# An attention and routed-MLP kernel: an eighth buffer for ScalarE's tiles, output rows scaled on GpSimd, another plan, and the routed rows stored by plain DMAs

## The chip, the cores and the metric

The kernel runs on one core of a Trainium2 chip. The metric is the device time of one execution in microseconds (us). The engines are TensorE (PE, with its weight loads as PEld), VectorE (DVE), ScalarE (ACT), GpSimd (POOL) and SyncE (SP, which here only issues DMAs).

## The reference

One transformer layer on 2048 rows of width 448 in bfloat16: attention with 16 heads that share one key and one value head of width 28, then an MLP that is applied to eight rows alone.

```python
def _A_ref(x, wq, wk, wv, wo):
    B, S, D = x.shape            # 1, 2048, 448
    H = 16; Dh = D // H          # 28
    q = (x @ wq).reshape(B, S, H, Dh).transpose(0, 2, 1, 3)
    k = x @ wk                   # one key head, one value head
    v = x @ wv
    scores = jnp.einsum("bhqd,bkd->bhqk", q, k) * (Dh ** -0.5)
    p = _softmax(scores, axis=-1)
    o = jnp.einsum("bhqk,bkd->bhqd", p, v)
    return o.transpose(0, 2, 1, 3).reshape(B, S, H * Dh) @ wo

def _B_ref(x, w_r, w_gate, w_up, w_down):
    r = x @ w_r
    idx = jnp.argsort(-r, axis=-1)[:, :8]          # eight rows with the largest r
    x_sel = the rows idx of x
    y = (_silu(x_sel @ w_gate) * (x_sel @ w_up)) @ w_down      # F = 1792
    y = y * _sigmoid(r[idx])
    return x + (y added to the rows idx)

h  = x + _A_ref(_layernorm(x), ...)
h2 = h + _B_ref(_layernorm(h), ...)
```

## The kernel before

**How the order comes about.** The program first collects all operations in a graph (`_Graph.op`), each with its engine, an assumed duration, a priority `prio`, and the tiles that it reads and writes. `_Graph.plan` then plays the engines through in that model and fixes the order of every engine's instructions. `emit` writes them out, with a semaphore wait wherever an operation needs one of another engine. On the chip each engine keeps to its order, so an instruction that waits holds all that stand behind it on its engine.

Two rules of `plan` matter here. On TensorE, the score products for ScalarE are marked `crit`. When one of them is due soon, another piece of work (a filler) may start before it only if it would end at most `SLACK` ns after the product is due; otherwise TensorE waits for the product if it is due within `WAIT` ns, and else starts a filler all the same:

```python
fit = [o for o in now if t + o.dur + 100.0 * (o.form != form) <= soon.ready + SLACK]
if fit:
    c = min(fit, key=lambda o: (o.prio, o.idx))
elif soon.ready - t < WAIT:
    c, s = soon, soon.ready
```

And operations that are called `lock` (some of VectorE's) are kept apart in time from those of GpSimd, all of which count as `lock`; a GpSimd operation also waits for the last such VectorE operation.

**The work.** There are 16 blocks (four groups of four heads by four groups of 512 query rows), each with 16 tiles of 128 keys. For a tile, TensorE makes scores into two pairs of PSUM banks (`qk`), an engine turns them into weights, and TensorE multiplies these with the values into the block's accumulator. Which engine does the weights is fixed by `TILES` (per block: its VectorE tiles, how many of them give one step to GpSimd, and an offset in time) and by `EARLY` for the first two blocks:

- A ScalarE tile is two pieces (`act_unit`). Each is one exponential of 128x1024 scores from PSUM into one of `NPB` buffers of `P` (L1012). One product with the values takes two buffers (`act_pv`). The score banks 0 and 1, 2 and 3 alternate.
- A VectorE tile is two pieces (`dve_unit`, L1024) from the banks 4 and 5, which write an integer form of the weights into `Y`, and three shifted copies of it (`shift`, L1031). The third copy goes to GpSimd for the first tiles of a block, as many as `TILES` says. Its product with the values (`dve_pv`) has four times as many matmuls as that of a ScalarE tile.

Beside these run, in the same loop: the projection of the next block's queries (`q_project`), of the keys and values of later rows (`chunk`), the normaliser of the last block by way of DRAM (`post_block`, its product with the output on GpSimd in L767), and for each 128 finished rows the output projection and the second layer norm (`out_proj`). For the row tiles 0 to 7 `out_proj` ends with the scaled output row (L802, VectorE) and a store of two row tiles. All matmuls are recorded under L436, so they are told apart by their operands.

**The tail.** After the last exponential come the last normaliser, projection and layer norm, the search for the eight rows, the gathering of their inputs by one-hot products, the MLP, and the eight new rows in `fin` (two half copies, L1236 on ScalarE and L1238 on VectorE). GpSimd then stores them with one indirect DMA (L1239), whose row numbers `idxc` lie on eight partitions. It waits for the earlier stores of output rows. Every engine also loads a flag into a register (L1284) and branches on it (L1295).

Of the kernel before, what the change touches and what calls it, by code (L numbers as in the profile page):

```python
# [12 lines left out]
I32 = mybir.dt.int32  # L13
U32 = mybir.dt.uint32
F16 = mybir.dt.float16

SLACK, WAIT = 248.0, 240.0
# [4 lines left out]
    2: ((0, 5, 8, 13), 4, -0.95),  # L22
    3: ((0, 3, 6, 10, 13), 3, 0.94),
    4: ((2, 8, 10, 12), 2, 1.48),
    5: ((1, 4, 6, 11), 0, 1.34),
    6: ((2, 6, 11, 13), 2, -0.37),
    7: ((1, 3, 8, 11, 13), 2, 1.13),
    8: ((4, 9, 11, 13), 0, 1.08),
    9: ((5, 7, 12), 3, 0.03),
    10: ((0, 5, 8, 10, 12), 3, 1.5),  # L30
    11: ((2, 4, 9, 12), 1, -0.68),
    12: ((0, 2, 4, 8), 4, 0.5),
    13: ((0, 2, 6, 9, 11), 5, 0.63),
    14: ((2, 10, 12), 3, 1.18),
    15: ((0, 4, 8, 10), 1, 0.33),
# [3 lines left out]
EARLY = [(0, 5, 18.21), (0, 15, 22.04), (0, 4, 23.54), (1, 12, 28.01)]  # L39
QUERY = {2: 12.3, 3: 12.3, 4: 6.9, 5: 7.0, 6: 11.5, 7: 11.1, 8: 8.7, 9: 10.4, 10: 6.7, 11: 9.5, 12: 10.1, 13: 7.6}  # L40
ROWS = {
    (0, 0): 10.9, (0, 1): 7.3, (0, 2): 10.3, (0, 3): 9.3, (1, 0): 10.7, (1, 1): 11.9, (1, 2): 13.1,
    (1, 3): 9.9, (2, 0): 6.2, (2, 1): 11.4, (2, 2): 8.4, (2, 3): 9.2
}
CHUNK = (0.0, 5.1, 10.9, 36.9)
# [7 lines left out]
class _Graph:  # L53
# [221 lines left out]
    def emit(self, eng, e, at=None):  # L275
        for o in self.orders[eng]:
# [9 lines left out]
            if w and not o.dma:  # L286
                hold = w.pop()
# [13 lines left out]
def _main(nc, G, sb, ps, psb, flag, scr, xs, ptab, A_x, A_wq, A_wk, A_wv, A_wo, B_w_r, B_w_gate, B_w_up, B_w_down, out,  # L301
# [8 lines left out]
    NPB = 6  # L310
# [12 lines left out]
    idi = sb("idi", [128, 128], I32)  # L323
# [45 lines left out]
    junk = sb("junk", [128, D], BF16)  # L369
    outf = x_sb[:, :, 0:D]  # L370
# [36 lines left out]
    idxc = sb("idxc", [8, 1], U32)  # L407
# [12 lines left out]
    eg = sb("eg", [128, NFC, 8], F32)  # L420
    sg = sb("sg", [128, NFC, 8], F32)
# [10 lines left out]
    def pk(b):  # L432
        return ("ps", b)
# [31 lines left out]
    G.op(PO, lambda e: e.iota(idi[:, :], [[1, 128]], base=0, channel_multiplier=-1), 250, writes=["idi"])  # L465
    G.op(PO, lambda e: e.tensor_single_scalar(ident[:, :], idi[:, :], 0, ALU.is_equal), 560,
         reads=["idi"], writes=["ident"])
# [40 lines left out]
    def kk(j, p):  # L508
        return ("K0", min(j, 2), p) if j < 4 else ("K", j // 4, p)
# [25 lines left out]
    def late_consts(gate):  # L535
# [16 lines left out]
        G.op(PO, lambda e: e.memset(onesb[:, :], 1.0), 200, writes=["onesb"])  # L552
        G.op(PO, lambda e: e.memset(bz[:, :, :], 0.0), 100, writes=["bz"])
        G.op(PO, lambda e: e.memset(onesh[:, :], 1.0), 200, writes=["onesh"])
# [6 lines left out]
        G.op(PO, lambda e: e.iota(idi[0:8, 0:96], [[1, 96]], base=0, channel_multiplier=0), 250, writes=["idi"])  # L561
        G.op(PO, lambda e: e.tensor_copy(iota96[:, :], idi[0:8, 0:96]), 300, reads=["idi"], writes=["iota96"])
# [7 lines left out]
        G.op(PO, lambda e: e.iota(idi[:, :], [[-32, 4], [0, 32]], base=0, channel_multiplier=1), 250, writes=["idi"])  # L570
# [209 lines left out]
    def out_proj(qb, k):  # L780
# [20 lines left out]
        if qb < 2:  # L801
            G.op(DV, lambda e: e.tensor_scalar(outf[:, t, :], h, st[:, t, 5:6], s6, ALU.mult, ALU.add), 420,  # L802
                 reads=[("h", hr), ("st5", t), ("h6", hr)], writes=[("outf", t)], lock=True)
# [216 lines left out]
    def dve_unit(m, b, j, p, t):  # L1020
        n = m % NY
        G.op(PE, qk(4, b, j, p), 216, reads=[("Q", b % 4), ("Qh", b % 4), kk(j, p)], writes=[pk(4), pk(5)], prio=t - 2.9,
             form=1)
        G.op(DV, lambda e: e.tensor_scalar(Y[:, n, 0, p:p + 3:2, :].bitcast(I16), ps[:, 4:6, :], 0.0,  # L1024
                                           32639.0 - 3 * STEP, ALU.max, ALU.min), 1140, reads=[pk(4), pk(5)],
             writes=[("Y", n, 0, p)], prio=t - 2)

    def shift(m, v, b):
# [18 lines left out]
    for m, (b, j, t) in enumerate(dve_tiles):  # L1047
        for p in range(2):
            at(t + 1.5 * p, dve_unit, m, b, j, p, t + 1.5 * p)
        for v in (1, 2, 3):  # L1050
            at(t + 1.6 + 0.5 * v, shift, m, v, b)
# [295 lines left out]
```

## Time and profile before

| | |
|---|---|
| time, median of 3 runs | 388.7 us (387.9 to 390.82) |
| time of the profiled execution | 387.67 us |
| its span, first to last instruction | 385.9 us |
| granted TensorE clock, mean | 0.984 |
| ScalarE busy | 374.1 us |
| TensorE busy | 344.0 us |
| VectorE busy | 338.2 us |
| GpSimd busy | 115.0 us |

How to read the lines. In a group of instructions stand the line of the kernel, the engine, the operation, output and input with their shapes, the count, then the busy time of the group, the mean duration of one instruction in ns, and the engine's idle time just before them with what ended it. Instructions overlap on an engine, so the busy time can be less than count times duration. The chain that ended last is followed back from the last instruction, and shown in order of time as start, duration and what ran. In the timeline a row has the start, the time from first start to last end of the merged instructions (x12 is twelve), and in brackets the idle time before them. A "q" behind an engine's name is its sequencer, which issues DMAs and loads registers. The row of a window gives its ends, its length, and the busy time and count of PE, PEld, DVE, ACT and POOL. An answer on one line gives for each engine the count, then the shortest, median and longest duration in ns, then the start of the first and of the last.

### The profile page before, as it was taken

The page shows a single profiled execution, that of the slowest core. Times are in us where ns is not written, and L with a number is a line of the kernel's source. Part 1 is how long each engine was busy: PE and PEld are TensorE (multiplying, and loading weights), DVE is VectorE, ACT ScalarE, POOL GpSimd, SP SyncE. Part 2 cuts the span into 40 slices and gives each one's busy share as a digit, 9 for nine tenths or more (in the row PEclk, how much of TensorE's full clock was granted, in tenths as well). Part 3 has the DMA queues.
Part 4 walks back from the last instruction along what each step waited for, and adds up shares of the span by engine and source line. Part 5 has one row for each costly group of instructions (what it writes and reads, how often), then busy time and mean ns, then how long its engine had stood idle before and what let it go on. Part 6 is the DMA issues. An engine that isn't in the chain of part 4 may idle for free.

```text
span 385.9 us, 8129 instructions
## 1 busy us (share of the span) xinstructions
PE 344.0 (89%) x3361; PEld 105.6 (27%) x3361; DVE 338.2 (88%) x613; ACT 374.1 (97%) x433; POOL 115.0 (30%) x149
## 2 busy tenths in 40 slices
PE   7799898989988999899998988999898999888945
PEld 7333222222222222222222222222222222222324
DVE  6985888888998999989999989999999998999382
ACT  6999999999999999999999999999999999999992
POOL 7440002544123112404101244402145454431100
PEclk9999999999999999999999999999999999999985
DMA  8696000100000000201001000011001010100011
GB/s 208 163 235 190 2 2 12 49 2 29 2 27 5 4 29 26 77 1 54 2 14 63 7 27 27 28 50 31 26 30 51 3 53 27 52 26 20 14 51 55
DMA packets 18045, 17.12 MB, mean 44 GB/s; under 512 B 6660, under 2 KB 15124, under 8 KB 18004
## 3 DMA queue, kind: packets, MB, share of 16 engines
q1 hardware_dynamic: 17652, 16.32, 14.7%
q8 instruction: 27, 0.44, 0.5%
q10 hardware_dynamic: 288, 0.23, 0.2%
q14 instruction: 14, 0.11, 0.1%
q0 software_dynamic: 64, 0.02, 0.0%
HBM read 11.70 MB, written 4.86 MB: 43 GB/s over the span
## 4 chain that ended last, share of the span: by engine, by line
ACT 92%; PE 3%; DVE 3%; DMA 1%; issue 0%; SPq 0%; POOL 0%; POOLq 0%
ACT P L1012 90%; PE ps L436 3%; DMA wq_sb<-in_A_wq_dram 1%; ACT xn L964 1%; DVE Y L1024 1%; DVE topb L856 0%; DVE bn L934 0%; SPq L449 0%; ACT x_sb L825 0%; DVE Y L1031 0%; ACT xnT L618 0%; POOL out_dram L1239 0%; ACT Rb L741 0%; ACT Rb L739 0%; ACT wq_pad L491 0%
## 5 line engine op out<-in xcount | busy, mean ns | idle before, releaser
L1012 ACT ACTIVATE P<-ps 128x1024 bf16<-128x1024 f32 x388 | 356.3, 1132 | 1.4 <-PE ps L436 1.3
L436 PE MATMUL ps<-Q,K 64*128 64x512 bf16 x1024 | 179.9, 385 | 29.3 <-ACT P L1012 25.0
L1024 DVE TENSOR_SCALAR Y<-ps 128x1024 int16<-128x1024 f32 x124 | 151.2, 1219 | 19.8 <-PE ps L436 19.5
L1031 DVE TENSOR_SCALAR Y<-Y 128x2048 int16<-128x2048 int16 x153 | 100.4, 685 | 0.5
L436 PEld LDWEIGHTS ps<-Q,K 64*128 64x128 bf16 x1024 | 44.7, 93 | 175.4 <-ACT P L1012 152.7
L1031 POOL TENSOR_SCALAR Y<-Y 128x2048 int16<-128x2048 int16 x33 | 62.6, 1898 | 96.4 <-DVE Y L1031 87.6
L436 PE MATMUL ps<-Y,Vs 128*32 128x512 bf16 x992 | 84.9, 383 | 0.0
L436 PE MATMUL ps<-P,Vs 128*32 128x512 bf16 x776 | 76.3, 388 | 0.1
L767 POOL TENSOR_TENSOR On<-Ot,Rb 128x512 bf16<-128x512 f32 x15 | 19.1, 1273 | 45.5 <-DVE Y L1031 30.6
L436 PEld LDWEIGHTS ps<-Y,Vs 128*32 128x32 bf16 x992 | 23.8, 95 | 27.3 <-issue 17.5
L436 PEld LDWEIGHTS ps<-P,Vs 128*32 128x32 bf16 x776 | 19.6, 93 | 42.5 <-issue 41.7
L763 POOL TENSOR_TENSOR Ls<-Ls,Lc 128x16 f32<-128x16 f32 x15 | 4.2, 280 | 68.2 <-DVE Y L1031 60.9
L436 PE MATMUL ps<-xnT,wq_pad 112*128 112x512 bf16 (+1 forms) x68 | 19.2, 371 | 0.6 <-DVE K L643 0.5
L436 PE MATMUL ps<-wo_pad,On 128*128 128x448 bf16 (+1 forms) x64 | 17.5, 358 | 1.0 <-DVE On L745 1.0
L517 DVE TENSOR_SCALAR Q<-ps,qone 128x512 bf16<-128x512 f32 x15 | 11.0, 734 | 1.7 <-PE ps L436 1.7
L795 POOL TENSOR_TENSOR hbuf<-st,nhalf 128x1 f32<-128x1 f32 x12 | 6.6, 552 | 14.3 <-DVE Y L1031 10.3
L751 DVE COPY Ot<-ps 128x512 f32<-128x512 f32 x15 | 10.3, 684 | 0.7 <-PE ps L436 0.4
L804 DVE SCALAR_TENSOR_TENSOR junk<-hbuf,w_rb 128x448 bf16<-128x448 f32 x12 | 8.1, 677 | 0.0
L789 DVE TENSOR_TENSOR hbuf<-ps,x_sb 128x448 f32<-128x448 f32 x12 | 7.4, 618 | 0.3 <-PE ps L436 0.2
L791 DVE BATCH_NORM_STATS2 bn<-hbuf 128x6 f32<-128x448 f32 x12 | 7.4, 618 | 0.1
L719 DVE TENSOR_SCALAR K<-ps,ksc,kb 128x512 bf16<-128x512 f32 x6 | 4.6, 803 | 3.3 <-PE ps L436 3.3
L1239 POOL DMA_INDIRECT out_dram<-wq_sb,idxc x1 | 0.9, 930 | 20.8 <-DVE wq_sb L1238 20.8
(209 smaller groups left out, 172.1 us busy)
## 6 DMA issues: line engine op xcount, KB each, us to landing
Rb<-h_scr SPq DMA_DIRECT2D x15, 256.0 KB
h_scr<-hbuf SPq DMA_DIRECT2D x12, 225.0 KB, 2.2
out_dram<-x_sb SPq DMA_DIRECT2D x8, 224.0 KB, 2.5
wg_sb<-in_B_w_gate_dram SPq DMA_DIRECT2D x1, 1568.0 KB, 12.2
wu_sb<-in_B_w_up_dram SPq DMA_DIRECT2D x1, 1568.0 KB, 18.7
wd_sb<-in_B_w_down_dram SPq DMA_DIRECT2D x1, 1568.0 KB, 22.1
x_sb<-in_A_x_dram SPq DMA_DIRECT2D x3, 448.0 KB, 5.6
wo_pad<-in_A_wo_dram SPq DMA_DIRECT2D x4, 98.0 KB
```

The source lines that it names most:

```text
L436: return lambda e: e.matmul(o, lhsT=l, rhs=r, start=start, stop=stop)
L517: G.op(DV, lambda e: e.tensor_scalar(Q[:, b % 4, :], ps[:, bank, :], qone[:, 0:1], None, ALU.add), dvt(512), reads=[pk(bank), "qone"], wri ...
L719: G.op(DV, lambda e, bank=bank, c=c, p=p: e.tensor_scalar(K[:, p, c * 512:(c + 1) * 512], ps[:, bank, :], ksc[:, p:p + 1], kb[:, p:p + 1], ...
L751: G.op(DV, lambda e: e.tensor_copy(Ot[:, rb, :], ps[:, acc_bank(b), :]), dvt(512), reads=[pk(acc_bank(b))], writes=[("Ot", rb)], prio=u - 30)
L767: G.op(PO, lambda e: e.tensor_tensor(On[:, qb % 2, g, :], Ot[:, rb, :], Rb[:, rb, :], ALU.mult), 1270, reads=[("Ot", rb), ("Rb", rb)], wri ...
L789: G.op(DV, lambda e: e.tensor_tensor(h, ps[:, bank, 0:D], x_sb[:, t, 0:D], ALU.add), dvt(D), reads=[pk(bank), ("x", t)], writes=[("h", hr)])
L791: G.op(DV, lambda e: e.bn_stats(bn6[:, t, :], h), dvt(D), reads=[("h", hr)], writes=[("bn6", t)])
L795: G.op(PO, lambda e: e.tensor_tensor(s4, st[:, t, 7:8], nhalf[:, 0:1], ALU.pow), 570, reads=[("st7", t), "nhalf"], writes=[("h4", hr)])
L804: G.op(DV, lambda e: e.scalar_tensor_tensor(junk[:, :], h, s4, w_rb[:, :], ALU.mult, ALU.mult, accum_out=st[:, t, 2:3]), 700, reads=[("h", ...
L1012: marks["exp"] = G.op(AC, lambda e: e.activation(P[:, sl, :, :], ps[:, b0:b0 + 2, :], ACT.Exp, bias=EBIAS, scale=OCT), 905, reads=[pk(b0), ...
L1024: G.op(DV, lambda e: e.tensor_scalar(Y[:, n, 0, p:p + 3:2, :].bitcast(I16), ps[:, 4:6, :], 0.0, 32639.0 - 3 * STEP, ALU.max, ALU.min), 114 ...
L1031: G.op(PO if po else DV, lambda e: e.tensor_scalar(Y[:, n, v, :, :].bitcast(I16), Y[:, n, 0, :, :].bitcast(I16), 1.0, v * STEP, ALU.mult, ...
```

## The change

- `NPB` goes from 6 to 8 buffers of `P`. To make room, `idi` is laid into `junk`, and `onesb`, `onesh`, `eg` and `sg` into `wq_sb`.
- `TILES`, `EARLY`, `QUERY`, `ROWS`, `CHUNK`, `SLACK` and `WAIT` have other values. The VectorE tiles in `TILES` are 60 instead of 58 (with four in `EARLY` each time), and those whose third copy goes to GpSimd are 45 instead of 33. The priorities of `dve_unit` and `shift` get offsets of their own, `PACE`, and the assumed duration of a copy on GpSimd goes from 2030 to 1930 ns.
- The scaled output rows of the row tiles in `POOLROWS` (seven of the eight) are made on GpSimd.
- The eight routed rows are stored by eight plain DMAs, four issued by SP and four by ScalarE. The byte offset of a row is made on one partition (`idxr`), loaded into registers of the two engines (`fetch`, after all earlier stores of output rows), and used as the address (`put`).

```diff
-SLACK, WAIT = 248.0, 240.0
+SLACK, WAIT = 144.0, 159.0
 TILES = {
-    2: ((0, 5, 8, 13), 4, -0.95),
-    3: ((0, 3, 6, 10, 13), 3, 0.94),
...
-    14: ((2, 10, 12), 3, 1.18),
-    15: ((0, 4, 8, 10), 1, 0.33),
+    2: ((0, 2, 6, 12), 4, -1.5),
+    3: ((0, 2, 6, 10, 13), 4, 0.75),
...
+    14: ((0, 3, 7, 11), 2, 0.98),
+    15: ((0, 4, 6, 11), 1, 0.84),
 }
...
+POOLROWS = [0, 1, 2, 3, 4, 5, 7]
+PACE = (-6.4, -1.8, 1.1, -3.6, 1.5, 2.8)
-CHUNK = (0.0, 5.1, 10.9, 36.9)
+CHUNK = (0.0, 6.3, 7.4, 13.5)
...
-            if w and not o.dma:
+            if w and not o.dma and o.name != "load":
                 hold = w.pop()
...
-    NPB = 6
+    NPB = 8
...
-    idi = sb("idi", [128, 128], I32)
+    idi = junk[:, 0:256].bitcast(I32)
-    idxc = sb("idxc", [8, 1], U32)
+    idxr = sb("idxr", [1, 8], I32)
-    onesb = sb("onesb", [128, 128], BF16)
+    onesb = wq_sb[:, 1, 0:128]
-    onesh = sb("onesh", [128, 128], F16)
+    onesh = wq_sb[:, 2, 0:128].bitcast(F16)
-    eg = sb("eg", [128, NFC, 8], F32)
-    sg = sb("sg", [128, NFC, 8], F32)
+    eg, sg = (wq_sb[:, 3, 224 * k:224 * k + 224].bitcast(F32).rearrange("p (c n) -> p c n", n=8) for k in range(2))
...
         if qb < 2:
-            G.op(DV, lambda e: e.tensor_scalar(outf[:, t, :], h, st[:, t, 5:6], s6, ALU.mult, ALU.add), 420,
-                 reads=[("h", hr), ("st5", t), ("h6", hr)], writes=[("outf", t)], lock=True)
+            on = t in POOLROWS
+            G.op(PO if on else DV, lambda e: e.tensor_scalar(outf[:, t, :], h, st[:, t, 5:6], s6, ALU.mult, ALU.add),
+                 900 if on else 420, reads=[("h", hr), ("st5", t), ("h6", hr)], writes=[("outf", t)], lock=True)
...
     def dve_unit(m, b, j, p, t):
-        G.op(PE, qk(4, b, j, p), 216, ..., prio=t - 2.9, form=1)
+        G.op(PE, qk(4, b, j, p), 216, ..., prio=t + PACE[0] + (PACE[2] - 1.5) * p, form=1)
-             writes=[("Y", n, 0, p)], prio=t - 2)
+             writes=[("Y", n, 0, p)], prio=t + PACE[1] + (PACE[2] - 1.5) * p)
-    def shift(m, v, b):
+    def shift(m, v, b, t):
-                                  1.0, v * STEP, ALU.mult, ALU.add), 2030 if po else 605,
+                                  1.0, v * STEP, ALU.mult, ALU.add), 1930 if po else 605,
-             writes=[("Y", n, v)], lock=True)
+             writes=[("Y", n, v)], lock=True, prio=t + PACE[2 + v])
...
-    ps3 = ps[0:8, 2, 480:482]
-    G.op(PE, [mm(ps3, oh5[:, k, :], x_sb[:, 12 + k, D:D + 2], k == 0, False) for k in range(4)] +
-         [mm(ps3, oh5[:, 4, :], extc[:, D:D + 2], False, True)], 200, ...)
-    G.op(DV, lambda e: e.tensor_copy(sel3[:, :], ps3[:, 1:2]), 70, ...)
-    G.op(DV, lambda e: e.tensor_tensor(idxc[:, :], ps3[:, 0:1], sel3[:, :], ALU.add), 70, ...)
+    lrow = ps[0:1, 2, 480:488]
+    G.op(PE, [mm(lrow, (x_sb[:, 12 + k, D + h:D + h + 1] if k < 4 else extc[:, D + h:D + h + 1]), oh5[:, k, :],
+                 k == h == 0, k == 4 and h == 1) for k in range(5) for h in range(2)], 280, ...)
+    G.op(DV, lambda e: e.tensor_scalar(idxr[:, :], lrow, 2.0 * D, None, ALU.mult), 70, ...)
...
-    o = G.op(PO, lambda e: e.indirect_dma_start(out[0], bass.IndirectOffsetOnAxis(ap=idxc[:, 0:1], axis=0),
-                                                fin[:, :], None), 1000, dma=True, ...)
-    evs.append(o)
+    out_b = out[0].rearrange("s d -> (s d)").bitcast(U8)
+    where = {}
+    def fetch(i):
+        def run(e):
+            got = nc.values_load_multi_w_load_instructions(
+                idxr[0:1, i:i + 4], engines=(e.engine,), min_val=0, max_val=(S - 1) * 2 * D, ...)[1]
+            where.update(zip(range(i, i + 4), got))
+        return run
+    def put(j):
+        return lambda e: e.dma_start(out_b[bass.ds(where[j], 2 * D)].unsqueeze(0), fin[j:j + 1, :].bitcast(U8))
+    outs = [("out", q, k) for q in range(4) for k in (1, 3)]
+    for i, eng in ((0, SP), (4, AC)):
+        o = G.op(eng, fetch(i), 500, reads=["idxr"] + outs, prio=329.8)
+        o.name = "load"
+        for j in range(i, i + 4):
+            evs.append(G.op(eng, put(j), 100, dma=True, reads=["fin0", "fin1"], writes=[("out", 4 + j)], prio=331, after=[o]))
```

More of the change, by code (lines that the diff above doesn't have):

```diff
@@ L1238, in _main @@
     G.op(DV, lambda e: e.tensor_copy(fin[:, hd:D], ps[0:8, 1, hd:D]), 300, reads=[pk(1)], writes=["fin1"])
-    o = G.op(PO, lambda e: e.indirect_dma_start(out[0], bass.IndirectOffsetOnAxis(ap=idxc[:, 0:1], axis=0),
-                                                fin[:, :], None), 1000, dma=True,
-             reads=["fin0", "fin1", "idxc"] + [("out", q, k) for q in range(4) for k in (1, 3)],
-             writes=[("out", 4)])
-    evs.append(o)
+    out_b = out[0].rearrange("s d -> (s d)").bitcast(U8)
[3 more added lines that the diff above has]
+            got = nc.values_load_multi_w_load_instructions(
+                idxr[0:1, i:i + 4], engines=(e.engine,), min_val=0, max_val=(S - 1) * 2 * D,
+                skip_runtime_bounds_check_because="a one-hot sum of the bytes ahead of a row below S")[1]
+            where.update(zip(range(i, i + 4), got))
[8 more added lines that the diff above has]
+            evs.append(G.op(eng, put(j), 100, dma=True, reads=["fin0", "fin1"], writes=[("out", 4 + j)], prio=331, after=[o]))
     G.close(evs, "flag")
```

54 lines of the change are left out of this document (26 added, 28 removed).

## The prediction

> **What bounds the kernel now.** I read the page's busy shares, its chain and its groups first, then the chain in order of time.
>
> ```profile
> span 385.9 us, 8129 instructions
> PE 344.0 (89%) x3361; PEld 105.6 (27%) x3361; DVE 338.2 (88%) x613; ACT 374.1 (97%) x433; POOL 115.0 (30%) x149
> ACT 92%; PE 3%; DVE 3%; DMA 1%; issue 0%; SPq 0%; POOL 0%; POOLq 0%
> L1012 ACT ACTIVATE P<-ps 128x1024 bf16<-128x1024 f32 x388 | 356.3, 1132 | 1.4 <-PE ps L436 1.3
> ```
>
> ScalarE (ACT) is busy 97% of the span, and 92% of the chain that ended last lies on it. Nearly all of that is one group, the exponential of line 1012: 388 pieces, 356.3 us, with 1.4 us of idle time before them. One piece lasts 1132 ns but overlaps its neighbour, so the pace is 356.3 / 388 = 0.918 us. The same view in order of time shows how whole this is:
>
> ```profile
> 9.47 59.75 ACT P L1012 x65
> 69.23 121.64 ACT P L1012 x133
> 190.91 148.97 ACT P L1012 x162
> ...
> 349.28 16.61 ACT P L1012 x18
> ```
>
> From 9.47 to 365.89 us ScalarE does exponentials and nothing else. What follows, up to 385.9, is a serial tail of 20.0 us. Once, between 339.88 (190.91 + 148.97) and 349.28, the chain leaves ScalarE, for PE and DVE. The remaining 388 - 378 = 10 pieces run there, in 9.40 us.
>
> The other engines in this loop, one row for the whole of it (PE, PEld, DVE, ACT, POOL busy), and ScalarE in its last undisturbed stretch:
>
> ```profile
> 9.47:365.88 356.41, 326.33 (x3033) 91.41 (x3031) 320.99 (x533) 356.27 (x389) 106.97 (x116) 1.00 0.14 40
> 355.68 10.20 ACT L1012 ACTIVATE P<-ps 128x1024 bf16<-128x1024 f32 x11
> ```
>
> DVE has 356.4 - 321.0 = 35.4 us to spare, PE 30.1, POOL 249. The stretch gives a pace of (10.20 - 1.13) / 10 = 0.907 us. So 388 x (0.918 - 0.907) = 4.3 us of the loop is score matmuls that came a little late.
>
> **The change, part by part.** *Fewer exponentials.* The key tiles on VectorE go from 62 (58 in the table, 4 early) to 64 (60 and 4). Each of the 256 tiles is two score pieces, so ScalarE has 384 instead of 388: 4 x 0.918 = **-3.67 us**, wholly on the path. The price is paid beside it:
>
> ```profile
> L1024 DVE TENSOR_SCALAR Y<-ps 128x1024 int16<-128x1024 f32 x124 | 151.2, 1219 | 19.8 <-PE ps L436 19.5
> L1031 DVE TENSOR_SCALAR Y<-Y 128x2048 int16<-128x2048 int16 x153 | 100.4, 685 | 0.5
> L1031 POOL TENSOR_SCALAR Y<-Y 128x2048 int16<-128x2048 int16 x33 | 62.6, 1898 | 96.4 <-DVE Y L1031 87.6
> L436 PE MATMUL ps<-Y,Vs 128*32 128x512 bf16 x992 | 84.9, 383 | 0.0
> L436 PE MATMUL ps<-P,Vs 128*32 128x512 bf16 x776 | 76.3, 388 | 0.1
> L436 PE MATMUL ps<-wo_pad,On 128*128 128x448 bf16 x48 | 13.1, 358 | 0.0
> L802 DVE TENSOR_SCALAR x_sb<-hbuf,st 128x448 bf16<-128x448 f32 x8 | 4.1, 508 | 0.0
> L699 POOL TENSOR_SCALAR xn<-x_sb,nmean,rstd 128x448 bf16<-128x448 bf16 x5 | 3.5, 713 | 1.1 <-DVE xn L695 0.8
> L767 POOL TENSOR_TENSOR On<-Ot,Rb 128x512 bf16<-128x512 f32 x15 | 19.1, 1273 | 45.5 <-DVE Y L1031 30.6
> ```
>
> DVE gets 4 more L1024 (4 x 151.2 / 124 = +4.9 us). The third shift of a tile goes to GpSimd for 45 tiles instead of 33, so DVE does 3 x 64 - 45 = 147 shifts instead of 153 (6 x 100.4 / 153 = -3.9) and GpSimd 12 more (12 x 1.898 = +22.8). PE gets 32 more Y products and 8 fewer P products (32 x 0.086 - 8 x 0.098 = +2.0 us), against 30.1 of idle time.
>
> *Output rows on GpSimd.* Seven of the eight L802 leave DVE: -3.6 us there. No row shows this operation on GpSimd with f32 input. From below stands L699 (the same operation and width, bf16 in, 0.713), from above L767 (two f32 inputs, 512 wide, 1.273). I take 0.8, near L699, which is alike in all but the input: 7 x 0.8 = +5.6. In the loop DVE comes to 318.4 and GpSimd to 135 of 352 us, so neither is near full and I cost both at nothing. A row that ends later delays its store on SP's queue, and behind that store stand the normaliser's transfers, which feed L767. PE stood idle for 0.0 us before the projections that read it (`wo_pad,On` above). If that cover went, 4 stores times the 0.3 us by which 0.8 exceeds 0.508 would cost 1.2 us.
>
> *Eighth buffer.* A P buffer comes free when its P product has run. At the end of the loop this row stands, just as the exponentials end:
>
> ```profile
> 365.85 0.61 PE L436 MATMUL ps<-P,Vs 128*32 128x512 bf16 x8
> ```
>
> Eight products are two tiles, four buffers: of six, two are free even there, and the page names only 1.3 us in which an exponential waited for PE at all. So the buffers take no wait away: 0. They let the plan put P products later, which belongs to the next part.
>
> *The plan.* PE's order is fixed beforehand. A filler (a product, a projection piece) may start if it would end no more than SLACK after the next score piece is due, 0.248 us before and 0.144 after. Otherwise PE idles if that piece is due within WAIT (0.240, now 0.159), else the filler starts all the same. Short fillers will therefore overrun less, long ones more often. How late a score then comes no row shows. From below all 4.3 us go, with 384 x 0.907. From above stands the rival on long pieces. I stay near the present pace and take **-0.6**, a seventh of that sum.
>
> *The tail.* What now follows the last copies:
>
> ```profile
> 381.16 0.35 ACT L1236 ACTIVATE wq_sb<-ps 8x224 bf16<-8x224 f32 x1 [2.77 <-PE ps L436]
> 381.50 0.38 DVE L1238 CAST wq_sb<-ps 8x224 bf16<-8x224 f32 x1 [0.44 <-PE ps L436]
> 382.45 0.93 POOL L1239 DMA_INDIRECT out_dram<-wq_sb,idxc  x1 [20.80 <-DVE wq_sb L1238]
> out_dram<-wq_sb,idxc POOLq DMA_INDIRECT x1, 2.9
> 2.77 0.49 SPq L449 DMA_DIRECT2D wv_sb<-in_A_wv_dram  x1
> 3.30 0.49 SPq L449 DMA_DIRECT2D wq_sb<-in_A_wq_dram  x1
> h_scr<-Li SPq DMA_DIRECT2D x15, 8.0 KB, 1.4
> Lc<-h_scr SPq DMA_DIRECT2D x16, 8.0 KB, 1.7
> h_scr<-hbuf SPq DMA_DIRECT2D x12, 225.0 KB, 2.2
> ```
>
> The rows are ready at 381.88. The indirect store begins 0.57 later and lands at 382.45 + 2.9 = 385.35, 0.5 before the end. Instead SP and ScalarE issue four stores each, one every 3.30 - 2.77 = 0.53 us, the last at 381.93 + 3 x 0.53 = 383.5. Landing takes 1.4 to 2.2 us by the small and the large transfers; with 1.7 it is 385.2: **-0.2**, bounds -0.5 and +0.3. No row shows a DMA whose address comes from a register. The addresses must be in registers by then, and the load of them waits for all earlier stores. On ScalarE the last copy L1236 stands behind that load; on SP only its own four stores do.
>
> ```profile
> L1284 ACTq TENSOR_LOAD <-flag x1: 552/552/552, 378.2 to 378.2; - x1
> L289 POOLq EVENT_SEMAPHORE  x31: 17/17/4824, 3.8 to 379.4; - x31
> ```
>
> GpSimd's wait for those same stores ends at 379.4. One load of 0.552 ends at 380.0, inside L1236's idle time of 2.77; four loads would end at 381.6 and push the copy 0.45 us late, but the copy beside it ends at 381.88 anyway, so at most +0.1. A register step ahead of each store is bounded by the 17 ns of a semaphore step in the second row and by a whole load, 0.552: four of them add 0.1 to 2.2 us on a queue. I take the first, since a step on registers moves no data, and it stays inside the rounding of -0.2; the upper bound of the tail becomes +2.6. The row index now takes ten small matmuls instead of five and one DVE step instead of two, while PE waits for the selected rows: nothing. The tiles laid into others' memory cost nothing, since each old use is long over.
>
> *The sum.* -3.67 - 0.6 - 0.2 = -4.5 us against the profiled execution's own 387.67, which lies 1.0 below the median of the runs, 388.7. The median after is **384.2**. A change under 1% (3.9 us) can't be told from none.
>
> **Rivals.** *The late scores go too*: with SLACK smaller, ScalarE runs at 0.907 all through. 388.7 - 3.67 - 4.3 - 0.2 = **380.5**. For it speaks that PE has idle time; against it that the long pieces stay long.
>
> *The plan eats the gain.* A long piece holds PE for about 0.54 us:
>
> ```profile
> 66.31 0.61 PE L436 MATMUL ps<-xnT,wq_pad 112*128 112x512 bf16 x2
> 66.85 0.39 PE L436 MATMUL ps<-Q,K 64*128 64x512 bf16 x2
> L436 PE MATMUL ps<-xnT,wq_pad 112*128 112x512 bf16 x60 | 18.2, 384 | 0.5 <-DVE K L643 0.5
> ```
>
> With WAIT smaller it may start 0.08 us nearer to a due score. These 60 and the 48 of `wo_pad,On` are 54 such pieces: 54 x 0.08 = +4.3, so 388.7 - 3.67 - 0.2 + 4.3 = **389.1**, no change. Against it: it wants every piece to meet the worst place.
>
> *GpSimd holds VectorE* (the slower side). A DVE instruction that meets a running GpSimd one can stand still until that ends:
>
> ```profile
> 344.45 1.90 POOL L1031 TENSOR_SCALAR Y<-Y 128x2048 int16<-128x2048 int16 x1 [3.11 <-DVE Y L1031]
> 344.54 1.83 DVE L856 CAST topb<-top 1x8 bf16<-1x8 f32 x1
> 347.42 0.15 DVE L857 CAST posf<-idx 1x8 f32<-1x8 uint32 x1
> ```
>
> A cast of eight numbers took 1.83 us, until GpSimd's shift was over; its neighbour took 0.15. This is where the chain left ScalarE, whose ten pieces took 9.40 instead of 9.07: 0.33 us lost. GpSimd will have 52 shifts and rows instead of 33. From 12 such collisions on (3.9 / 0.33) the gain is gone, from 24 the kernel is over 1% slower; with 26, half of them, 388.7 - 3.9 + 8.6 = **393.4**. Against it: the plan keeps the instructions that it calls `lock` apart, and among 33 shifts only this undeclared cast was caught whole. [...]
>
> *The stores queue up.* If SP's and ScalarE's issues took turns, the eighth would start at 381.93 + 7 x 0.53 = 385.6 and land at 387.3, 2.0 after today's: 388.7 - 4.3 + 2.0 = **386.4**. Against it stand two queues at work at once at the start, each at 0.44 us an issue:
>
> ```profile
> 0.84 0.88 SPq L449 DMA_DIRECT2D x_sb<-in_A_x_dram  x2
> 0.72 0.89 ACTq L449 DMA_DIRECT2D x_sb<-in_A_x_dram  x2
> ```
>
> [...]
>
> **How the numbers follow.** The forecast has 0.48 (its own range 382.5 to 386.5), late scores gone 0.18, gain eaten 0.18, GpSimd's hold 0.11, queued stores 0.05. Faster by over 1% (below 384.8) is 0.18 and two thirds to three quarters of 0.48: 0.52. Slower by over 1% is most of GpSimd's case: 0.10. Within 1%: 0.38. The range reaches from 380.0, under the second case, to 390.0, over the third, and leaves out most of the fourth.
>
> **What would show it.** L1012 x384 at 0.915 to 0.918 us; L1031 x147 on DVE and x45 on POOL, L1024 x128, one L802-like group x7 on POOL near 0.8 us; the last landing within 0.5 us of 3.3 after the copies, with no GpSimd step. A pace over 0.925 says that the plan or GpSimd took the gain: casts or shifts on DVE well over their medians name GpSimd, long pieces ahead of late scores the plan. A load of registers that holds L1236, or eight stores strictly in turn, would prove the tail wrong.

## The result, and the profile after

The changed kernel takes **385.4 us** (median of 4 runs, 384.72 to 385.91) against 388.6 before on the same chip: a ratio of 0.9922, interval 0.990 to 0.9944. That is 3.2 us, or 0.8%. The profiled execution took 385.39 us, 2.28 less than the one of before. From the page of the changed kernel come its span, busy shares, granted clock in 40 slices, the chain's shares and five groups:

```profile
span 383.6 us, 8231 instructions
PE 355.0 (93%) x3390; PEld 105.4 (27%) x3390; DVE 340.0 (89%) x603; ACT 370.3 (97%) x429; POOL 141.2 (37%) x166
PEclk9999999999996999999999999999999999999975
ACT 92%; PE 5%; DVE 1%; issue 0%; POOL 0%; POOLq 0%
L1014 ACT ACTIVATE P<-ps 128x1024 bf16<-128x1024 f32 x384 | 352.6, 1195 | 1.8 <-PE ps L438 1.8
L1026 DVE TENSOR_SCALAR Y<-ps 128x1024 int16<-128x1024 f32 x128 | 155.8, 1217 | 17.9 <-PE ps L438 16.3
L1033 POOL TENSOR_SCALAR Y<-Y 128x2048 int16<-128x2048 int16 x45 | 85.4, 1898 | 103.7 <-DVE Y L1033 103.7
L1033 DVE TENSOR_SCALAR Y<-Y 128x2048 int16<-128x2048 int16 x147 | 100.6, 709 | 0.7
L804 POOL TENSOR_SCALAR x_sb<-hbuf,st 128x448 bf16<-128x448 f32 x7 | 5.0, 715 | 15.5 <-DVE Y L1033 12.3
```

ScalarE is still what bounds the kernel: 97% busy, 92% of the chain. There are 384 exponentials, and their pace, 352.6 / 384 = 0.918 us, is that of before. New is a slice of the clock row that reads 6, or 0.6 of full speed. Before, the row had no such slice ahead of the tail:

```profile
PEclk9999999999999999999999999999999999999985
```

The chain of the changed kernel in order of time shows what lies there:

```profile
9.55 14.77 ACT P L1014 x16
24.34 63.35 ACT P L1014 x69
87.70 30.36 ACT P L1014 x33
118.07 0.05 issue
118.11 2.15 PE ps L438 x10
120.28 1.03 ACT P L1014
121.31 0.05 issue
121.36 3.00 PE ps L438 x16
124.38 68.50 ACT P L1014 x75
192.91 24.18 ACT P L1014 x26
217.09 145.86 ACT P L1014 x159
```

The loop of exponentials runs from 9.55 to 217.09 + 145.86 = 362.95, with a stop near 118 to 124 us where TensorE ends last. Before, the only such stop was at 340. The windows view of the whole loop and of that place (columns: ends, length, busy time and count of PE, PEld, DVE, ACT and POOL, then the granted clock as a share):

```profile
9.55:362.94 353.39, 337.05 (x3057) 91.09 (x3055) 322.65 (x524) 352.64 (x385) 134.08 (x134) 0.99 0.14 40
116.00:126.00 10.00, 8.83 (x58) 1.85 (x62) 9.29 (x16) 9.28 (x11) 2.92 (x2) 0.66 0.07 26
```

The loop took 353.39 us instead of 356.41, so 3.02 less. The granted clock was 0.66 in the 10 us around the stop: full speed fell to half (0.51) from 117.3 to 124.2. Behind the loop, the time to the end grew from 19.97 to 20.64. The rows of the tail (timeline; then the last branch of ScalarE, and the drain that it executes behind it, with count, durations in ns and start):

```profile
375.68 0.65 PE L438 MATMUL ps<-xselT,wu_sb 112*128 112x8 bf16 x19 [0.32 <-issue]
378.67 0.35 ACT L1236 ACTIVATE wq_sb<-ps 8x224 bf16<-8x224 f32 x1 [3.23 <-PE ps L438]
379.42 1.81 ACTq L1251 DMA_DIRECT2D out_dram<-wq_sb  x4
379.41 1.33 SPq L1251 DMA_DIRECT2D out_dram<-wq_sb  x4
L1310 ACTq COMPARE_BRANCH  x1: 72/72/72, 381.3 to 381.3; - x1
L1266 ACTq DRAIN  x1: 66/66/66, 383.3 to 383.3; - x1
```

SP and ScalarE issue their four stores side by side, and the last landing comes at 382.24, 2.85 after the copies, where it was 3.48 before. But the kernel does not end there. ScalarE branches at 381.25 and goes on only at 383.30, so the end lies 1.35 us after the last landing; before it was 0.50. What the stores won was lost again.

### The profile page after: what moved, and what is told of

It reads as the page before. It is cut to its first block, busy times and chain, and to the rows that moved or that the text cites. A ratio compares the mean times of both kernels' runs of the same rounds, so it can differ in the third digit from the quotient of the medians.

```text
span 383.6 us, 8231 instructions
## 1 busy us (share of the span) xinstructions
PE 355.0 (93%) x3390; PEld 105.4 (27%) x3390; DVE 340.0 (89%) x603; ACT 370.3 (97%) x429; POOL 141.2 (37%) x166
## 4 chain that ended last, share of the span: by engine, by line
ACT 92%; PE 5%; DVE 1%; issue 0%; POOL 0%; POOLq 0%
ACT P L1014 91%; PE ps L438 5%; ACT xn L966 1%; DVE bn L936 0%; ACT x_sb L827 0%; PE ps L441 0%; ACT Rb L742 0%; ACT Rb L740 0%; POOL ident L468 0%; DVE On L746 0%; DVE wq_sb L1238 0%; DVE mv L937 0%; POOL junk L467 0%; DVE x_sb L957 0%; DVE Li L756 0%
## 5 line engine op out<-in xcount | busy, mean ns | idle before, releaser
L1014 ACT ACTIVATE P<-ps 128x1024 bf16<-128x1024 f32 x384 | 352.6, 1195 | 1.8 <-PE ps L438 1.8
L1026 DVE TENSOR_SCALAR Y<-ps 128x1024 int16<-128x1024 f32 x128 | 155.8, 1217 | 17.9 <-PE ps L438 16.3
L1033 POOL TENSOR_SCALAR Y<-Y 128x2048 int16<-128x2048 int16 x45 | 85.4, 1898 | 103.7 <-DVE Y L1033 103.7
L1033 DVE TENSOR_SCALAR Y<-Y 128x2048 int16<-128x2048 int16 x147 | 100.6, 709 | 0.7
L438 PE MATMUL ps<-Y,Vs 128*32 128x512 bf16 x1024 | 91.0, 385 | 0.0
L438 PEld LDWEIGHTS ps<-Y,Vs 128*32 128x32 bf16 x1024 | 22.6, 94 | 35.3 <-issue 32.6
L768 POOL TENSOR_TENSOR On<-Ot,Rb 128x512 bf16<-128x512 f32 x15 | 19.1, 1274 | 23.5 <-DVE Y L1033 10.7
L804 POOL TENSOR_SCALAR x_sb<-hbuf,st 128x448 bf16<-128x448 f32 x7 | 5.0, 715 | 15.5 <-DVE Y L1033 12.3
L764 POOL TENSOR_TENSOR Ls<-Ls,Lc 128x16 f32<-128x16 f32 x15 | 3.3, 219 | 20.1 <-DVE junk L896 11.6
```

The source lines that it names most:

```text
L438: return lambda e: e.matmul(o, lhsT=l, rhs=r, start=start, stop=stop)
L768: G.op(PO, lambda e: e.tensor_tensor(On[:, qb % 2, g, :], Ot[:, rb, :], Rb[:, rb, :], ALU.mult), 1270, reads=[("Ot", rb), ("Rb", rb)], wri ...
L804: G.op(PO if on else DV, lambda e: e.tensor_scalar(outf[:, t, :], h, st[:, t, 5:6], s6, ALU.mult, ALU.add), 900 if on else 420, reads=[("h ...
L1014: marks["exp"] = G.op(AC, lambda e: e.activation(P[:, sl, :, :], ps[:, b0:b0 + 2, :], ACT.Exp, bias=EBIAS, scale=OCT), 905, reads=[pk(b0), ...
L1033: G.op(PO if po else DV, lambda e: e.tensor_scalar(Y[:, n, v, :, :].bitcast(I16), Y[:, n, 0, :, :].bitcast(I16), 1.0, v * STEP, ALU.mult, ...
```

## Experiments

**The changed kernel once more**, as the measure for the others.

> The changed kernel itself, beside the kernel before. My theory of the 3 us it gained: four exponentials fewer give -3.67 us, the plan's late scores give and take the same (short fillers -1, long pieces +1), a stretch of lower granted clock near 118 us costs 1.2 us in the profiled execution, and the tail is 0.7 us longer. If the low clock was an accident of that execution, the profile here shows none and a span near 382.4; if it belongs to the new order, it is there again at the same place with a span near 383.6. Median 3 us below before either way.

Measured: 385.83 us (12 runs), ratio 0.9927 [0.9907, 0.9947]. Its profile has a loop of 353.66 and a tail of 20.06, with the clock at half of full speed (half clock, from here on) twice, at 119.3 to 122.8 and 344.6 to 348.0.

**The stores alone**: the tail of before in the changed kernel, one indirect DMA with the row numbers on eight partitions.

```diff
-    for i, eng in ((0, SP), (4, AC)):   # registers, eight stores
+    o = G.op(PO, lambda e: e.indirect_dma_start(out[0], ...))
```

> The changed kernel with the old end: one row index per partition, one indirect DMA on GpSimd; all other engines' orders are the same. Theory: the eight stores land 0.6 us sooner after the copies than the indirect one, but the end of the program then waits about 0.8 us for ScalarE, so the two ends cost the same within 0.3 us: 385.4 +- 0.3. Rival: the longer tail of the changed kernel is the new stores' doing, so this one is 0.7 us faster, 384.7. Second rival: the stores are a gain that something else in the tail hides, so this one is 0.6 slower, 386.0.

Measured: 385.0 us (384.84 to 385.61, 4 runs), ratio 0.9912 [0.9893, 0.9931]. Its tail is 20.04 us, that of the eight stores 20.06 and 20.64 in the two profiles above: the new stores gain nothing over the old one. (The medians are 0.4 to 0.8 us apart, but three of these four runs had a mean clock of 0.979 or more; runs of the changed kernel with such a clock are as fast, see the low clock below.) Its branch needs no 2 us:

```profile
L1297 ACTq COMPARE_BRANCH  x1: 68/68/68, 378.5 to 378.5; - x1
L1253 ACTq DRAIN  x1: 80/80/80, 379.0 to 379.0; - x1
116.00:126.00 10.00, 6.99 (x64) 1.68 (x63) 9.88 (x20) 10.00 (x12) 2.08 (x2) 1.00 0.07 26
```

In the same execution the clock stayed full around 120 us (third row, windows view), and the loop took 352.46, about 1 us less. The edit has no part in that stretch, and the two profiles of the changed kernel differ in their half clock too, so the low clock comes in some executions of this order and not in others.

**Four exponentials twice**: four of the 384 are also written to an unused tile.

```diff
+        twice = (b, j, p) in ((4, 6, 0), (7, 7, 0), (10, 6, 0), (13, 7, 0))
+        fe = [exponential into a spare tile] * twice + [exponential into P]
```

> The changed kernel in its own order, with four of the 384 exponentials (one each in blocks 4, 7, 10 and 13) done twice, the first time into memory that nothing reads then. ScalarE has 388 pieces again, and nothing is taken from VectorE or TensorE. If ScalarE's pieces lie wholly on the path: +4 x 0.903 = +3.6 us on the changed kernel. If part of them is hidden by waits for scores (rival): +1 to +2.5 us.

Measured: 388.32 us (12 runs), ratio 0.9991 [0.9975, 1.0008]. The loop:

```profile
10.15:367.27 357.12, 336.44 (x3057) 90.68 (x3055) 322.15 (x524) 356.32 (x389) 134.30 (x134) 1.00 0.13 39
L1313 ACTq COMPARE_BRANCH  x1: 73/73/73, 385.0 to 385.0; - x1
L1269 ACTq DRAIN  x1: 65/65/65, 385.5 to 385.5; - x1
```

It is 3.73 us over that of the changed kernel and 3.46 over its repetition. Four exponentials are worth 0.87 to 0.93 us each. These loops differ in their half clock; more direct is the start of the piece behind each repeated one, which came 0.90 to 0.93 us late. So they lie wholly on the path. The median rose by 2.5 only; in the profile the tail fell to 19.31, as here ScalarE went on 0.50 us after its branch (384.96 to 385.46). That was not expected, and it became the lead for the end.

**The buffers alone**, eight instead of six, in before's order and with its tail.

```diff
-    NPB = 6
+    NPB = 8        # and the tiles laid into others' memory; plan and tail of before
```

> The kernel before with eight instead of six P buffers and the small tiles laid into others' memory, and nothing else: the order of TensorE, ScalarE, VectorE and SyncE is that of before. Theory: no exponential waited for a buffer, so no change, 388.6 +- 0.4. Rival: buffers were waited for in a few places that the idle time does not show, 0.25 to 0.6 us, or more: 387 to 388.

Measured: 388.49 us (11 runs), ratio 1.0001 [0.9984, 1.0017]. Its loop in the windows view and its exponentials on the page:

```profile
10.10:366.50 356.40, 326.32 (x3033) 91.34 (x3031) 320.79 (x533) 356.27 (x389) 107.39 (x115) 1.00 0.13 39
L1014 ACT ACTIVATE P<-ps 128x1024 bf16<-128x1024 f32 x388 | 356.3, 1134 | 1.4 <-PE ps L438 1.3
```

356.40 against 356.41: without another order the two more buffers are worth nothing.

**Six buffers under the new plan's values.** The planner then has to find its order with six.

```diff
-    NPB = 8
+    NPB = 6
```

> The changed kernel with six P buffers instead of eight, and all else as it is; the plan is made anew for six, with the same numbers. The buffers alone, in the order of before, were worth nothing. If the eight buffers matter only through the order that they allow (theory), this order is worse: an exponential has to find its buffer free, products must come sooner and scores come late, +3 to +7 us on the changed kernel. If they don't matter even so (rival): within 1 us of it.

Measured: 389.06 us (10 runs), ratio 1.0013 [1.0001, 1.0025].

```profile
9.69:366.47 356.78, 332.45 (x3057) 91.62 (x3055) 322.01 (x524) 354.82 (x385) 134.28 (x135) 1.00 0.14 39
```

With 384 exponentials the loop takes 356.78, or 3.4 us more than with eight buffers, spread over some 13 scores late by more than 0.25 us each. So buffers and plan go together: two more remove no wait from the old order, but the new values lose all they gain without them. Values chosen for six buffers and 384 exponentials were not tried, so what the buffers are worth beside the best order with six stays open.

**ScalarE's end, first theory**: the mark that announces the branch, moved from the middle of ScalarE's program to 12 operations before its end.

```diff
-    at = {lst[0 if eng in (PO, SP) else len(lst) // 2].idx: [hint]}
+    at = {lst[0 if eng in (PO, SP) else len(lst) - 12 if eng == AC else len(lst) // 2].idx: [hint]}
```

> The changed kernel with ScalarE's branch hint, which names the target of its last branch, placed 12 operations ahead of ScalarE's end instead of in the middle of its work. In the changed kernel ScalarE goes on 1.8 to 2.05 us after that branch, in the kernel before 0.48, and the program ends with it. If the target has to be fetched anew because the hint is long past (theory), ScalarE goes on 0.5 us after the branch, the end comes 0.5 us after the last landing and the tail is 0.6 to 0.8 us shorter than the changed kernel's 20.06 to 20.64: median 385.1. If ScalarE waits for its own four stores instead (rival), it still goes on 2 us after the branch and nothing changes.

Measured: 385.98 us (6 runs), ratio 0.9931 [0.9915, 0.9947].

```profile
L1310 ACTq COMPARE_BRANCH  x1: 73/73/73, 381.7 to 381.7; - x1
L1266 ACTq DRAIN  x1: 66/66/66, 384.0 to 384.0; - x1
```

The delay is still there (381.67 to 383.97). The theory fell.

**Second theory, the number of ScalarE's stores**: six on SP, two on ScalarE.

```diff
-    for i, eng in ((0, SP), (4, AC)):
+    for i, eng, n in ((0, SP, 6), (6, AC, 2)):
```

> The changed kernel with six of the eight stores on SyncE and two on ScalarE instead of four and four. SyncE's issues came 0.35 us apart, so its last store starts 0.7 us later and lands near 3.4 to 3.5 us after the copies instead of 2.85; ScalarE branches 0.7 us sooner. If ScalarE's late going on sets the end (theory), the end moves with it: 0 to 0.6 us shorter, and the last landing is again 0.5 us ahead of the end. If the last landing sets it (rival): 0.6 us longer.

Measured: 385.88 us (6 runs), ratio 0.9927 [0.9911, 0.9942].

```profile
L1251 ACTq DMA_DIRECT2D out_dram<-wq_sb x2: 249/386/523, 380.0 to 380.9; - x2
L1310 ACTq COMPARE_BRANCH  x1: 72/72/72, 381.2 to 381.2; - x1
L1266 ACTq DRAIN  x1: 66/66/66, 383.9 to 383.9; - x1
```

ScalarE reaches its branch two stores earlier in its program and still goes on no sooner: the wait behind the branch grew to 2.65. So it is not the branch that the delay counts from. The first row holds the clue: two stores 0.92 us apart. In the run with four exponentials twice, where ScalarE went on 0.50 us after its branch, the first two stood 0.62 apart (383.42 and 384.04). In all nine profiles with 0.92 us ScalarE goes on 2.45 to 3.22 us after the second store, with four stores or with two.

**The low clock, first try**: 32 score products around the two stretches in which TensorE has least to do, issued twice.

```diff
+THIN = [*range(108, 123), *range(354, 371)]
-        G.op(PE, qk(b0, b, j, p), 216, ...)
+        G.op(PE, qk(b0, b, j, p) * (2 if n in THIN else 1), 216, ...)
```

> The changed kernel in its own order, with the score products of 32 ScalarE pieces (15 from about 108 us, 17 from about 334 us) made twice, which changes no result. In the changed order TensorE has two stretches of over 3.4 us, near 114 and 340 us, in which it works about 0.35 of the time (0.40 or more everywhere in the kernel before), and the granted clock fell to half right after them in two of three profiles. If thin work brings the low clock about (theory): no half-clock stretch inside the loop, loop 352.3 to 352.8 us as in the profile without one, 0.6 to 1.2 us less than the changed kernel. If the low clock has another cause (rival): half-clock stretches appear as often as before. If the doubled products delay ScalarE instead: a loop longer than 353.7.

Measured: 388.36 us (12 runs), ratio 0.9997 [0.9984, 1.001].

```profile
10.00:366.00 356.00, 340.84 (x3123) 91.68 (x3119) 322.63 (x525) 354.33 (x385) 134.17 (x134) 1.00 0.14 39
```

The clock stays full, but the loop is 2.6 us longer: most doubled products outside the thin stretches came 0.18 us late, those inside next to nothing. (The windows below have TensorE busy for 0.60 of such a stretch; the 0.35 of the expectation is in no view.)

**The low clock, second try, and four empty instructions on ScalarE.** Ten products instead of 32; four empty instructions at the head of ScalarE's program; both.

```diff
+THIN = [*range(115, 120), *range(362, 367)]        # the second and the third
+    for _ in range(4 if eng == AC else 0):          # the first and the third
+        e.nop()
```

> The changed kernel with four empty instructions at the head of ScalarE's program, and nothing else. Theory A (the place of ScalarE's last instructions in its instruction stream is what costs: the changed kernel shows a gap of 0.9 us instead of 0.3 between ScalarE's first and second store, and 1.8 to 2.7 us between its last branch and the instruction behind it, where the kernel with the four repeated exponentials, which has four ScalarE instructions more, showed 0.3 and 0.50): the last landing to the end falls from 1.1-1.6 us to about 0.5 us, the span behind the last exponential from 20.1-20.9 to about 19.3 us, the median from 385.8 to about 385.1 us. Theory B (something else in that kernel, such as its later and longer loop, made the end short): the branch to the next instruction stays at 1.8 us or more and the median stays at 385.6 to 386.0 us.

> The changed kernel with the score products of ten pieces (units 115 to 119 and 362 to 366, those that fall into the two thin stretches of TensorE's work near 114-117 and 340-344 us) issued twice, into the same banks, the second overwriting the first with the same values. The earlier run that doubled 32 of them lost 0.18 us on each doubled piece outside the thin stretches, and nothing on those inside. Theory A (the half clock comes from the thin stretches and costs about 1.1 us of the loop): no clock below full between 30 and 355 us, the loop of exponentials at 352.3 to 352.8 us in place of 353.4 to 353.8, the median near 384.9 us. Theory B (the half clock costs nothing that counts, or comes from elsewhere): the granted clock still falls to half near 119 or 345 us, or the loop stays at 353.4 us or more and the median at 385.6 to 386.0 us.

> Both edits at once: the four empty instructions on ScalarE and the ten score products issued twice. If both theories hold and the two add up: loop 352.3 to 352.8 us, the span behind the last exponential about 19.3 us, the median about 384.2 us, which would be 1.6 us under the changed kernel. If only one of them holds, 384.9 to 385.2 us; if neither, 385.6 to 386.0 us.

Measured, on one chip with before at 389.03: empty instructions 385.44 us (6 runs), ratio 0.9904 [0.9888, 0.992]; ten products 385.97 us (5), 0.992 [0.9905, 0.9935]; both 385.58 us (6), 0.9922 [0.9904, 0.994]. The empty instructions left no trace: ScalarE has 455 instructions, as without them. So the first is another repetition of the changed kernel and the third one of the second. For the clock (first row the third kernel, then the loops of the third and of the second, and two rows of the second from around 350 us, a DMA with its KB and us to landing and a row of the timeline):

```profile
116.00:126.00 10.00, 8.05 (x74) 2.01 (x74) 9.77 (x17) 10.00 (x12) 3.16 (x2) 1.00 0.07 26
9.51:362.02 352.51, 336.60 (x3077) 91.22 (x3075) 322.49 (x525) 352.48 (x385) 134.34 (x134) 1.00 0.14 40
10.50:363.90 353.40, 336.74 (x3077) 91.64 (x3075) 322.69 (x524) 352.75 (x385) 133.37 (x134) 1.00 0.14 39
h_scr<-Li SPq DMA_DIRECT2D x1, 8.0 KB, 3.2
357.38 0.56 PE L439 MATMUL ps<-wo_pad,On 128*128 128x450 bf16 x2 [0.70 <-POOL On L769]
```

The clock was full in both, and the mean clock was 0.979 or more in all 11 runs. One loop is 352.51 as hoped; the other lost 0.81 us at one piece near 358. That piece is none of the doubled ones. A transfer of the normaliser (`h_scr<-Li`) took 3.20 us there, 1.41 or 1.42 at this place in the 13 other profiles, and GpSimd's product and the projection behind it held the score (last two rows). In the same execution the last store of whole rows landed at 379.32, in the others of this length at 376.5 to 377.3, so the register load behind it began at 379.4 and pushed the copy. Why these transfers were slow no run shows. The ten doubled pieces themselves came 0.46 us late in sum, in both profiles. The medians did not fall. The theory holds for the cause of the low clock (full in both profiles, half in seven of the eight with the pieces made once) and not, in the medians, for its price.

**ScalarE's end, third theory**: eight instructions more, ahead of the first exponential.

```diff
+    first = next(o for o in lst if o.dur == 905)
+    at.setdefault(first.idx, []).append(lambda e: [e.wait_ge(sems[PE], 1) for _ in range(16)])
```

> The changed kernel with sixteen waits on ScalarE, on a semaphore value that is long reached, packed into eight instructions ahead of the first exponential, where ScalarE stands idle for 1.08 us. (The run with four empty instructions tested nothing: its trace has 455 instructions on ScalarE, as the changed kernel has, so it is a repetition of it.) From the traces so far: between ScalarE's first and second store lies a gap of 0.3 us with a code fetch in it, and the instruction behind the last branch comes 2.5 to 3.6 us after that gap in all profiles that have it, with four stores or with two; where four more exponentials put the step ahead of the first store, it came 0.50 us after the branch. Theory A (ScalarE steps into a new block of code between two stores, and its jump to the end is fetched anew after that step): with eight instructions more the step falls into the idle time ahead of the register load near 376.5 us; first and second store stand 0.62 us apart in place of 0.92, the next instruction comes about 0.5 us after the branch, last landing to end is about 0.5 us in place of 1.1 to 1.6, the span behind the last exponential 19.2 to 19.6 us in place of 20.1 to 20.9, and the median about 384.9 us. Theory B (the end waits for something else): branch to the next instruction 1.5 us or more, and the median 385.4 to 386.0 us, as in the three runs of the changed kernel.

Measured: **384.3 us** (383.35 to 384.73, 4 runs) against 388.66 before, ratio **0.9879 [0.986, 0.9899]**: the lowest median here.

```profile
379.86 1.51 ACTq L1251 DMA_DIRECT2D out_dram<-wq_sb  x4
L1313 ACTq COMPARE_BRANCH  x1: 73/73/73, 381.4 to 381.4; - x1
L1266 ACTq DRAIN  x1: 64/64/64, 381.9 to 381.9; - x1
10.29:363.71 353.42, 336.04 (x3057) 90.81 (x3055) 323.17 (x524) 352.67 (x385) 133.87 (x134) 1.00 0.14 39
```

The first two stores now stand 0.62 us apart, the drain comes 0.50 after the branch, and the end 0.55 after the last landing. The tail is 19.22 us, the loop as in the changed kernel (353.42). In the profile the gain is the tail's: from the last copy to the end it takes 3.09 us, against 3.80 to 4.46 in the nine profiles with 0.92 us between the stores. The median owes a part to the clock: three of these four runs have a mean clock of 0.98 or more, and with a clock of 0.979 or more the changed kernel's median is 384.73, theirs 384.19. So the place of ScalarE's last instructions in its stream decides here, as expected (drain 2.05 us behind the branch in the changed kernel, 0.50 now). That it is a step into a new block of code is a reading, not shown: blocks of 8192 and of 16384 bytes come in on two instruction queues, and in the changed kernel one of each begins in the gap between the stores (380.22 and 380.29) but is still under way when the second store starts (380.34). The trace doesn't say which engine a block is for.

## Why the prediction was right, and where its terms were not

**Fewer exponentials, -3.67**: right. The four repeated ones cost 3.46 to 3.73 us. The counts beside it came as listed: 128 of L1026, 147 and 45 of L1033. TensorE's price did not: its busy time in the loop rose by 10.7 us (337.05 - 326.33), by 8.5 in the execution with the old tail and full clock, and not by 2.0. It still had 16.3 us to spare, so the sum doesn't feel it.

**Output rows on GpSimd, 0**: right. L804 took 0.715 us, next to the lower bound of 0.713, not 0.8. VectorE is busy 322.65 us in the loop instead of 318.4. Of these 4.25 us, 4.1 lie in its shifts (100.6 instead of 100.4 - 3.9 = 96.5), whose mean went from 685 to 709 ns; some were held by GpSimd (below). TensorE still stood idle for 0.0 us before the 48 `wo_pad,On` products, so the cover that the working feared for held.

**The eighth buffer, 0** (six become eight, so it is two): right for the buffers by themselves (356.40 against 356.41). The place to which the working put its worth, the plan, is where the six-buffer run found it.

**The plan, -0.6**: this term was mis-sized, it came out at +0.65 (353.39 - 356.41 + 3.67). Its direction was read rightly in both parts. Counted piece by piece from the trace (start to start, over 0.903 us), short fillers held scores for 2.2 us before and 1.1 after, long pieces for 1.5 and 2.4; the two nearly cancel. On top came the half clock, some 1.1 us in this execution, which no step of the working had. With the old tail, where the clock stayed full, the same term is 352.46 - 356.41 + 3.67 = -0.28: the sign that was forecast, and half its size.

**The low clock.** TensorE's order after the change has a stretch in which it does little, near 114 to 117 us and again near 340 to 344. Windows of 3.40 us, the length of the second half clock of the repetition (344.6 to 348.0), in the changed kernel, in the one with the old tail, and one of the thinnest in the loop of before:

```profile
114.00:117.40 3.40, 2.03 (x16) 0.59 (x16) 3.40 (x11) 3.40 (x5) 0.00 (x0) 0.99 0.09 33
114.60:118.00 3.40, 2.17 (x18) 0.49 (x14) 3.40 (x11) 3.40 (x5) 0.00 (x0) 1.00 0.06 19
336.80:340.20 3.40, 2.34 (x19) 0.68 (x15) 3.40 (x9) 3.40 (x5) 0.76 (x1) 1.00 0.18 68
```

Half clock for 3.4 or 6.8 us behind such a stretch was in seven of the eight profiles with this order (all but the old tail's), and in none of the six of other orders or with the products doubled. The busy time of such a window doesn't tell by itself: 2.17 of 3.40 us kept full clock with the old tail, and so did 2.02 in the changed kernel itself, from 340.40 to 343.80. Why the clock falls in one execution and not in another no run shows. What it costs stays open too. Profiled loops with full clock took 352.46 and 352.51 us (a third, with the slow transfer, 353.40), those with half clock 353.4 to 354.0, leaving out the run that repeats exponentials. Of the 22 runs of the changed kernel (its own and the two repetitions), five had a mean clock of 0.979 or more, with a median of 384.73; the other 17 stand at 385.82. That says 1.1 us, if roughly, as the mean also depends on when the half clock of the tail begins (366.8 to 373.4 us in the profiles). But the kernels with ten products doubled, which never lost the clock, stand at 385.97 and 385.58. The doubled pieces give back some 0.46 us, and one slow transfer explains one execution; the rest of the difference no run explains.

**The tail, -0.2**: mis-sized, +0.67 in the profiled execution. Its parts: stores on two queues some 0.35 us apart instead of 0.53, one load of 0.50 to 0.52 us for four registers inside the idle time of the copy, and a register step of 29 to 43 ns ahead of each store, near the end of the bounds that was taken (17). The last landing came 2.85 us after the copies, not 3.3. So far it was better than worked out. What the working left out is ScalarE's own end: it took the 0.5 us from the last landing to the end for granted, whatever ScalarE has to do. With four stores and a load added to ScalarE's program it didn't (2.05 us behind its branch), and 0.85 us went. Another 0.32 is TensorE standing still on "issue" at 375.36 during the gathering, which is in some executions of both tails (7.5 or 7.8 to 8.1 us from the one-hot step to the copies). What ScalarE waits for behind its branch no run shows, nor why the same branch is over in 0.5 us when eight instructions more stand far ahead of it.

**The sum, -4.5**, was -2.28 between the two profiled executions and -3.2 between the medians: -3.67 + 0.65 + 0.08 (a later start) + 0.67 = -2.27. So the forecast of 384.2 lies near 385.4 because its one large term held; the two small ones missed the same way, by 1.25 and 0.87 us, and the gain of over 1% to which the working gave 0.52 did not come. With eight instructions more on ScalarE the medians differ by 4.4, the size that was forecast; that is in part luck, as it is not by the terms of that sum and three of its four runs had a high mean clock.

**The rivals.** *Late scores gone* needs 0.907 us a piece and met 0.918. *The plan eats the gain* has its mechanism in the long pieces, for 0.9 us and not 4.3. *Stores in turn*: the two queues' rows start at 379.41 and 379.42 side by side. *GpSimd holds VectorE* came true in its mechanism. The timeline of the changed kernel has the same sum twice, once beside GpSimd's product:

```profile
118.76 0.62 DVE L904 SCALAR_TENSOR_TENSOR junk<-x_sb,w_rb 128x448 bf16<-128x448 bf16 x1
119.92 1.27 POOL L768 TENSOR_TENSOR On<-Ot,Rb 128x512 bf16<-128x512 f32 x1 [6.81 <-DMA Rb<-h_scr]
120.44 1.23 DVE L904 SCALAR_TENSOR_TENSOR junk<-x_sb,w_rb 128x448 bf16<-128x448 bf16 x1
```

0.62 and 1.23 us. Such holds add up to some 5 us of VectorE, against 2.7 before, but it has 353.39 - 322.65 = 30.7 us to spare, and no exponential could be tied to one.

## What to carry to other kernels

Work taken from the engine that bounds the loop counted in full here (four exponentials, 3.5 to 3.7 us), while the smaller terms beside it, order and tail, may come out with the other sign: size them by bounds, and follow every engine to its last instruction, not only the last transfer. An engine that got more instructions near its end is worth a run with a few harmless ones ahead: eight took 0.7 to 1.4 us off the end here. When a new order leaves TensorE with little to do for some microseconds, read the granted clock there (0.66 over 10 us here) before reading the waits.

## What the runs showed of the hardware

- The granted clock fell to half for 3.4 or 6.8 us behind stretches in which TensorE was busy for some 60% of 3.4 us (2.03 of 3.40), but not behind every one: 2.02 of 3.40 kept its clock at another place of the same execution, 2.17 in another execution of the same order.
- ScalarE went on 1.5 to 2.7 us after its last branch in the nine profiles in which its first two stores stood 0.92 us apart, and 0.5 us after it in the two with 0.62 us and the three without stores on ScalarE. Four exponentials or eight waits more ahead of the stores moved it from the first case to the second.
- Two engines issued stores with addresses from registers side by side: in the changed kernel SP's four started 0.32 to 0.43 us apart, ScalarE's 0.92, 0.34 and 0.32. Two engines loaded their registers at the same time: four and four took 0.50 and 0.52 us, two and six 0.69 and 0.95.
